# K and V caches in one array read in tiles across borders, and layer 1's output projection in other tile sizes with unread products between

## The chip, the cores and the metric

The kernel runs on one core of one Trainium2 chip. The metric is the device time of one execution in microseconds (us), the median of several runs. Before the change it is 847.03 us, the median of 3 runs that lie between 846.56 and 848.1.

## The reference, cut to what matters

Two decoder layers with the same weights, one new token for each of 8 batches. A layer is attention over a cache of 4096 positions (32 query heads, 4 K/V heads of 128), then an MLP with a GELU.

```
x = x + A(layernorm(x))      # B=8, Sq=1, D=1024
x = x + M(layernorm(x))
x = x + A(layernorm(x))      # the same K, V and weights a second time
x = x + M(layernorm(x))

A(x): q = (x @ wq) as [8, 32, 1, 128];  k, v = caches [8, 4, 4096, 128], each K/V head for 8 query heads
      softmax(q k^T * 128**-0.5) v, heads side by side, @ wo        # wo [4096, 1024]
M(x): gelu(x @ w1 + b1) @ w2 + b2                                   # w1 [1024, 3584], w2 [3584, 1024]
```

All of it is float32. The two caches are 67 MB each and are read once in each layer.

## The kernel before

**The arena.** One buffer in on-chip memory, `arena`, holds everything that comes from memory. It is cut into 52 places of `SCW` = 1024 columns (128 x 1024 float32, 512 KB). Place 51 belongs to the softmax rows; in layer 0 places 0 to 27 hold `wq`, which the end of layer 0 uses again for layer 1's queries.

**The stream.** `stream` is a list, written out by hand, of every transfer of the program: how many places, from where in memory, and at which place of the arena it goes. `pump` walks it in order and issues each entry on SP's queue as soon as its places have been given back; SP is the only engine that issues these transfers, so an entry that has no place holds back all behind it. `release` gives a tile's places back after the last product that reads them. The transfers themselves run one behind the other.

**Attention.** `plan` goes through the batches; for each batch 8 pieces of K (`scores`, 2 places each), then the softmax (`probs`), then 8 pieces of V (`values`, 2 places each). `ap_of` finds the piece in the tile that holds it. In layer 0 the batches go 0 to 7, in layer 1 they go 7 to 0, so that the V of batch 7 (`shared`) stays on the chip between the layers. K and V are two arrays; a tile is 8 or 4 places (4 or 2 pieces) of one batch's K or V and starts and ends at a border of K or V. In layer 0 the tiles move through places 28 to 47, in layer 1 mostly as tiles of 8 through places 18 to 41.

**Output projection.** `project` multiplies the heads' outputs with `wo`. One place of `wo` is one head: four products of 256 columns into the four strips of the sum `y`, which the trace shows as 8 rows, since a product in float32 is two rows there. In layer 0 `wo` comes in tiles of 3 places and after each tile `idle` puts products on TensorE whose result nobody reads. In layer 1 it comes in tiles of 8, 8, 8, 4, 2 and 2 places, and nothing is put between.

**Unread products.** `idle` and `unread` do the same: `unread(n)` issues n products of 512 columns into one strip of 32 partitions of a PSUM tile that is called `none`. Before the change it is called only at the start of layer 1's attention (two after each of four K pieces, four in `probs`).

**MLP of layer 1.** After `project` and `layernorm` the program calls `expand("i1", ...)`: `w1` comes in tiles of 4 places; 4 places are one group u of 512 hidden columns (the products of line 317, from u = 5 on line 320). The variance (the products of line 211) is computed half way through group 0; the result of a group is scaled on ScalarE (line 335), transposed on TensorE (line 413), added up on VectorE, put through GELU, and multiplied one group later with `w2` (line 497, `down_row`), all of which is on the chip but for three last pieces (`LATE`). The sum is added to the residual on VectorE (line 872) and written out.

Of the kernel before, what the change touches and what calls it, by code (L numbers as in the profile page):

```python
# [8 lines left out]
F32 = mybir.dt.float32  # L9
# [5 lines left out]
P = 128  # L15
# [10 lines left out]
NG = W // CH  # L26
T = CH // P
NR = NH * HKV
EPS = 1e-5
PAD = 24  # L30
SCALE = DH ** -0.5
# [21 lines left out]
LATE_AT = 20  # L53
LATE_C = 2
LATE = ((0, 2), (2, 1), (3, 1))
NGR = F // CH
# [56 lines left out]


@with_exitstack
def decode_layers(ctx: ExitStack, tc: tile.TileContext, x, kc, vc, wq, wo, w1, w2, out):


    nc = tc.nc
# [75 lines left out]
            nc.tensor.matmul(ps[0:32, 0:w], ident[:, 0:32], ap[:, 0:w], start=True, stop=True)  # L195

    def unread(n):
        idle(*[CH] * n, ps=ps_o.tile([P, CH], F32, tag="o", name="none"), ap=arena.ap)

    turns = {}  # L200

# [231 lines left out]
    def project(name, lhs, resid, rsum, hooks={}):  # L433
        y = ps_o.tile([P, CH], F32, tag="o", name="y")
        n = 0
        for slot in tiles((name,)):
            for c in range(0, slot.cols, D):
                for j in range(4):
                    nc.tensor.matmul(y[32 * j:32 * j + 32, 0:Q4], lhs[:, n * B:n * B + 32],  # L439
                                     slot.ap[:, c + j * Q4:c + (j + 1) * Q4],  # L440
                                     start=(n == 0), stop=(n == HQ - 1))
# [12 lines left out]

# [219 lines left out]

    def ap_of(key):

        parts = pieces[st["layer"], key] if (st["layer"], key) in pieces else pieces[0, key]
        chunks = [held[name].ap[:, c:c + CH] for name, c0, n in parts for c in range(c0, c0 + n, CH)]
        return chunks, [name for name, c0, n in parts if c0 + n == held[name].cols]

    def plan(order):

# [61 lines left out]
            stream.append(((name, i0 + i), k, dram[:, at:at + n], starts(k, i), keys))  # L744
            at += n

    def lane(layer, b, a, r, m):
        where = k_at if a == "k" else v_at
        keys = [(a, *where(b, e)) for e in range(r, r + m)]
        for e, key in enumerate(keys):  # L750
            pieces[layer, key] = [((layer, keys[0]), e * W, W)]
        return (layer, keys[0]), (kc if a == "k" else vc)[b][:, r * W:(r + m) * W]

    def cache(layer, b, a, at):
        r = 0
        while r < NR:
            n, starts = at(2 * (NR - r))
            name, src = lane(layer, b, a, r, n // 2)
            yield (name, n, src, starts, ())
            r += n // 2  # L760

    rsum = row_sums()
    nc.vector.tensor_reduce(rsum, x_row, AX.X, ALU.add)

    last_b = B - 1
    shared = (("v7", 1, 44), ("v7b", 7, 28), ("v7c", 4, 35), ("v7d", 4, 39))
    orders = [list(range(B)), list(range(B))[::-1]]

    def fixed(*at):
        return lambda k, i: (at[i],)  # L770
# [8 lines left out]
    def listed(*spots):  # L779
        spots = iter(spots)  # L780
        return lambda left: next(spots)

    def batch(layer, b, k_spots, v_spots):
        for a, spots in [(a, spots) for a, spots in (("k", k_spots), ("v", v_spots)) if spots]:
            stream.extend(cache(layer, b, a, listed(*((n, (at,)) for n, at in spots))))
# [3 lines left out]
    batch(0, 0, ((8, 40), (4, 32), (4, 36)), ((4, 28), (8, 40), (4, 32)))  # L789
    batch(0, 1, ((4, 36), (4, 28), (8, 40)), ((8, 32), (8, 40)))  # L790
    cycle = [(((8, 36), (4, 44), (4, 28)), ((8, 32), (8, 40))), (((8, 28), (4, 36), (4, 40)), ((4, 44), (8, 28), (4, 36))),
             (((8, 40), (8, 28)), ((4, 36), (8, 40), (4, 28))), (((8, 32), (8, 40)), ((8, 28), (4, 36), (4, 40))),
             (((4, 44), (8, 28), (4, 36)), ((8, 40), (8, 28)))]
    for b in orders[0][2:last_b]:
        batch(0, b, *cycle[(b - 1) % 5])
    batch(0, last_b, cycle[(last_b - 1) % 5][0], ())
    at = 0
    for name, k, to in shared:
        keys = [(1, name, e) for e in range(k)] if at else ()
        stream.append(((0, name), k, vc[last_b][:, at:at + k * SCW], (to,), keys))  # L800
        for e in range(k):
            key = ("v", *v_at(last_b, (at + e * SCW) // W))
            pieces.setdefault((0, key), []).append(((0, name), e * SCW, SCW))
            pieces.setdefault((1, key), []).append(((1, name, e), 0, SCW) if keys else ((1, name), 0, SCW))
        at += k * SCW
# [4 lines left out]
    stream.append(((1, "v7"), 1, vc[last_b][:, 0:SCW], (17,), ()))  # L810
    batch(1, last_b, ((2, 20), (2, 22), (4, 24), (2, 18), (2, 20), (2, 22), (2, 24)), ())
    batch(1, last_b - 1, ((2, 26), (2, 18), (4, 20), (2, 24), (2, 28), (4, 30)), ((8, 34), (8, 18)))
# [12 lines left out]
    for layer in range(2):  # L825
        st["layer"] = layer
        b2_row = spare[:, SCW:SCW + Q4]
        hooks = {("probs", last_b): opened} if layer == 0 else {
            ("v", *v_at(last_b - 2, 0)): lambda: bias_row(b2_row, spare[:, SCW + Q4:SCW + Q4 + CH]),
            ("v", *v_at(last_b - 1, 1)): rebuild,  # L830
            ("v", *v_at(last_b - 3, 0)): bias_diag,
            **{("k", *k_at(last_b, r)): lambda: unread(2) for r in range(NR - 4, NR)}}
        last = attention(orders[layer], hooks)
        rsum = row_sums()
        project(f"o{layer}", oT, x_row, rsum, {4: last})
        rs = layernorm(x_row, rsum)
        if layer == 0:
            idle(CH)
            expand("i0", rs)
            idle(CH, Q4)  # L840
            swap()
        else:
            nc.vector.tensor_tensor(x_row, x_row, b2_row, ALU.add)
            y = []
# [27 lines left out]
            nc.vector.tensor_tensor(x_row, x_row, y[0], ALU.add)  # L872
# [14 lines left out]
    return w.reshape(1, -1, P, D).transpose(0, 2, 1, 3).reshape(1, P, -1)  # L887


def _tiles(n):  # L890
    return [t for j in range(4) for t in range(j, n, 4)]

# [20 lines left out]
def _start(x, b1, b2):  # L913
# [3 lines left out]

_LAYOUT = {
    'x': (('A_x', 'B_b1', 'B_b2'), _start),
    'k': (('A_k_cache',), lambda a: a.reshape(B, HKV, 4, 32, NH, W // DH, DH).transpose(0, 6, 4, 1, 2, 5, 3).reshape(B, P, -1)),  # L920
    'v': (('A_v_cache',), lambda a: a.reshape(B, HKV, P, -1).transpose(0, 2, 1, 3).reshape(B, P, -1)),
    'wq': (('A_wq',), _queries),
    'wo': (('A_wo',), _down),
    'w1': (('B_w1',), _across),
# [24 lines left out]
```

## Time and profile before

| | |
|---|---|
| median of 3 runs | 847.03 us (846.56 to 848.1) |
| profiled execution | 849.2 us, its span from first to last instruction 847.3 us |
| mean granted TensorE clock | 0.827 of full speed |
| busy: TensorE, its weight loads, VectorE, ScalarE | 66%, 22%, 23%, 7% of the span |
| bytes read | 356.21 MB, 421 GB/s over the span |

A row of a timeline gives the start and the length in us, the engine (PE is TensorE, PEld its weight loads, DVE VectorE, ACT ScalarE, SP SyncE), the line of the kernel, the operation, the tile written and those read, the shape, the number of instructions, and in brackets the idle time before it with what ended it. A row of windows gives a stretch, its length, for each engine the busy time and the number of instructions, then the granted clock of TensorE (1.00 is full speed), the mean busy share of the 16 DMA engines, and GB/s. A row of the chain gives start, length, and what the end of the program was waiting for in that time.

### The profile page before, as it was taken

What the parts mean: (1) busy time and instruction counts of PE and PEld (TensorE: products, weight loads), DVE (VectorE), ACT (ScalarE), POOL (GpSimd) and SP (SyncE); (2) the same over time, 40 slices, a digit from 0 to 9 for tenths busy, and PEclk for the clock granted to TensorE, in tenths of its full rate; (3) what the DMA queues carried; (4) which work ended last, traced back from release to release, by engine and by line L of the source; (5) the groups of instructions that cost most, each with busy time, mean ns of one, the idle gap of its engine ahead of it and who ended that gap; (6) DMA issues with size and microseconds to landing.
All of it is one profiled execution on the core that took longest, in us unless ns stands there. A gap on an engine that the chain in (4) does not pass through costs nothing.

```text
span 847.3 us, 9962 instructions
## 1 busy us (share of the span) xinstructions
PE 557.7 (66%) x4350; PEld 188.9 (22%) x4350; DVE 193.4 (23%) x642; ACT 55.9 (7%) x118; POOL 2.4 (0%) x14
## 2 busy tenths in 40 slices
PE   0756475566656647688988796576765566665778
PEld 0211121111111112133244322121211111112335
DVE  0013131313223231300010343231314132222011
ACT  0110000000000000000210200000000000000021
POOL 0000000000000000000000000000000000000000
PEclk9977778867787877799999998867688877878679
DMA  9999999999999999999999999999999999999997
GB/s 402 420 424 429 433 422 425 438 425 434 422 430 438 422 439 420 418 414 416 411 407 411 411 409 432 435 429 431 429 433 428 435 431 428 435 425 431 424 425 283
DMA packets 21066, 356.97 MB, mean 421 GB/s; under 512 B 2336, under 2 KB 2720, under 8 KB 4256
## 3 DMA queue, kind: packets, MB, share of 16 engines
q1 hardware_dynamic: 20880, 356.20, 99.0%
q8 instruction: 34, 0.56, 0.3%
q10 hardware_dynamic: 144, 0.15, 0.1%
q14 instruction: 8, 0.07, 0.0%
HBM read 356.21 MB, written 0.13 MB: 421 GB/s over the span
## 4 chain that ended last, share of the span: by engine, by line
DMA 68%; PE 28%; DVE 1%; issue 1%; another core or an unknown queue 1%; ACT 0%; SPq 0%; ACTq 0%; DVEq 0%
DMA arena<-in_k_dram 27%; DMA arena<-in_v_dram 24%; PE sps L612 8%; PE o_ps L657 8%; DMA arena<-in_w_dram 6%; DMA arena<-in_wo_dram 6%; DMA arena<-in_wq_dram 5%; PE acc L376 2%; PE acc L317 2%; PE sps L497 1%; PE y L439 1%; PE sps L484 1%; PE none L195 1%; PE sps L669 1%; PE acc L320 1%
## 5 line engine op out<-in xcount | busy, mean ns | idle before, releaser
L612 PE MATMUL sps<-arena,qz 128*32 128x512 f32 x1024 | 168.7, 801 | 120.2 <-DMA arena<-in_k_dram 119.1
L657 PE MATMUL o_ps<-arena 128*32 128x512 f32 x512 | 88.6, 811 | 44.3 <-DMA arena<-in_v_dram 32.8
L657 PE MATMUL o_ps<-arena,spare 128*32 128x512 f32 x512 | 81.4, 746 | 37.4 <-DMA arena<-in_v_dram 35.1
L612 PEld LDWEIGHTS sps<-arena,qz 128*32 128x32 f32 x1024 | 38.7, 136 | 211.0 <-issue 176.4
L662 DVE SCALAR_TENSOR_TENSOR scr<-o_ps,bits,scr 128x128 f32<-128x128 f32 x192 | 67.4, 351 | 6.8
L660 DVE TENSOR_SCALAR scr<-o_ps,bits 128x128 f32<-128x128 f32 x64 | 22.5, 351 | 135.9 <-PE o_ps L657 135.9
L439 PE MATMUL y<-arena,oxT 128*32 128x256 f32 x512 | 38.4, 444 | 18.1 <-DMA arena<-in_wo_dram 18.1
L669 PEld LDWEIGHTS sps<-bits,scr 128*128 128x128 f32 x128 | 22.0, 216 | 70.1 <-issue 49.1
L376 PE MATMUL acc<-arena,oxT 128*32 128x512 f32 x248 | 33.2, 664 | 6.5 <-DMA arena<-in_wq_dram 4.2
L657 PEld LDWEIGHTS o_ps<-arena 128*32 128x32 f32 x512 | 17.2, 134 | 79.3 <-issue 49.3
L195 PE MATMUL sps<-spare,ident 128*32 128x512 f32 (+2 forms) x82 | 33.9, 533 | 1.1 <-DVE scr L231 0.6
L670 DVE TENSOR_TENSOR oxT<-sps,scr 128x8 f32<-128x8 f32 x64 | 10.6, 165 | 101.1 <-PE sps L669 101.1
L617 DVE TENSOR_SCALAR_CACHE_REDUCE arena<-sps 128x512 f32<-128x512 f32 x16 | 11.1, 692 | 90.8 <-PE sps L612 90.8
L657 PEld LDWEIGHTS o_ps<-arena,spare 128*32 128x32 f32 x512 | 17.2, 125 | 65.4 <-issue 45.4
L638 ACT ACTIVATE sps<-arena,bits 128x512 f32<-128x512 f32 x16 | 10.9, 681 | 283.5 <-DVE scr L632 283.5
L617 DVE TENSOR_SCALAR_CACHE_REDUCE spare<-sps 128x512 f32<-128x512 f32 x16 | 11.1, 692 | 79.8 <-PE sps L612 79.8
L317 PE MATMUL acc<-arena,oxT 128*32 128x512 f32 x160 | 26.7, 675 | 3.8 <-DMA arena<-in_w_dram 3.8
L638 ACT ACTIVATE sps<-spare,bits 128x512 f32<-128x512 f32 x16 | 10.9, 681 | 266.1 <-DVE scr L632 266.1
L669 PE MATMUL sps<-bits,scr 128*128 128x8 f32 x128 | 27.9, 290 | 0.0
L439 PEld LDWEIGHTS y<-arena,oxT 128*32 128x32 f32 x512 | 17.2, 126 | 40.6 <-DMA arena<-in_wo_dram 24.0
L626 PE MATMUL sps<-scr,bits 128*128 128x128 f32 x32 | 7.4, 312 | 21.4 <-DVE scr L622 21.4
L220 PE MATMUL sps<-ident,xb 128*128 128x128 f32 x6 | 1.5, 344 | 24.2 <-DMA xb<-in_x_dram 23.2
(138 smaller groups left out, 285.3 us busy)
## 6 DMA issues: line engine op xcount, KB each, us to landing
arena<-in_v_dram SPq DMA_DIRECT2D x24, 4096.0 KB, 21.9
arena<-in_k_dram SPq DMA_DIRECT2D x22, 4096.0 KB, 21.3
arena<-in_k_dram SPq DMA_DIRECT2D x15, 2048.0 KB, 18.2
arena<-in_v_dram SPq DMA_DIRECT2D x10, 2048.0 KB, 18.6
arena<-in_wo_dram SPq DMA_DIRECT2D x10, 1536.0 KB, 9.8
arena<-in_w_dram SPq DMA_DIRECT2D x10, 1536.0 KB, 8.5
arena<-in_w_dram SPq DMA_DIRECT2D x12, 1024.0 KB, 9.8
arena<-in_w_dram SPq DMA_DIRECT2D x6, 2048.0 KB, 21.9
```

What stands on the lines that cost most here:

```text
L195: nc.tensor.matmul(ps[0:32, 0:w], ident[:, 0:32], ap[:, 0:w], start=True, stop=True)
L317: nc.tensor.matmul(acc[32 * j:32 * j + 32, :], lhs, slot.ap[:, c:c + CH], start=(kt < 4), stop=(kt >= NT - 4))
L376: nc.tensor.matmul(acc[u][32 * j:32 * j + 32, d0 - j * CH:d1 - j * CH], xnT[:, kt * XS:kt * XS + 32], ap[:, d0 - c0:d1 - c0], start=(kt == ...
L439: nc.tensor.matmul(y[32 * j:32 * j + 32, 0:Q4], lhs[:, n * B:n * B + 32], slot.ap[:, c + j * Q4:c + (j + 1) * Q4], start=(n == 0), stop=(n ...
L612: nc.tensor.matmul(ps[32 * g:32 * g + 32, :], qz[:, c:c + 32], kt[g], start=(j == 0), stop=(j == HKV - 1))
L617: nc.vector.tensor_scalar(st["row", b].ap[:, half * CH:(half + 1) * CH], ps, SCALE, None, op0=ALU.mult, op1=ALU.max, accum_out=st["mx", b] ...
L638: nc.scalar.activation(pp, row[:, h * CH:(h + 1) * CH], AF.Exp, bias=bias, scale=1.0, accum_out=ls[:, h:h + 1])
L657: nc.tensor.matmul(o[32 * g:32 * g + 32, :], s[:, g], v[g], start=(half == 0), stop=(half == NH - 1))
L660: nc.vector.tensor_scalar(r, o[:, 0:P], sel_t[:, 0:1], None, op0=ALU.mult)
L662: nc.vector.scalar_tensor_tensor(r, o[:, t * P:(t + 1) * P], sel_t[:, t:t + 1], r, op0=ALU.mult, op1=ALU.add)
L669: nc.tensor.matmul(po[:, 0:REP], r_s[j % 2], sel_h, start=True, stop=True)
L670: nc.vector.tensor_tensor(oT_v[:, j * REP:(j + 1) * REP, b], po[:, 0:REP], rl_s[b % 2][:, j * REP:(j + 1) * REP], ALU.mult)
```

## The change

K and V are one array `kv`: row p holds batch after batch that partition's K and then its V, 256 places in all, and behind them one place of zeros that no transfer reads. `cache` cuts this row into tiles without regard to the borders of pieces, of K and V, or of batches; `pieces` notes for each piece which places of which tiles hold it, and a tile is given back after the last piece that it has a part of.

- Layer 0: tiles of 8, 7 and 8 places in turn at places 36, 44 and 28 (23 places against 20), then 2, 1, 7, 4 and 4.
- Layer 1: the batches go 7, 0, 1, ..., 6, so that the array is read upwards. After the same first tiles as before come tiles of 9, 9 and 8 places in turn at 34, 17 and 26 (26 places against 24).
- Layer 1's `wo`: tiles of 8, 8, 8, 6 and 2 at 34, 17, 26, 34 and 40. After the third tile (24 heads) stand ten unread products, after the fourth (30 heads) two, and behind the layernorm four.
- `w1` in layer 1 has its old sizes at other places, `LATE` lies at place 22 instead of 20.

```
+            elif n < HQ:
+                unread({3 * HQ // 4: 10, HQ - 2: 2}.get(n, 0))
...
-    orders = [list(range(B)), list(range(B))[::-1]]
+    orders = [list(range(B)), [last_b, *range(last_b)]]
...
+    low, mid, high = (8, 28), (8, 36), (7, 44)
+    g = cache(0, 0, [mid, high, low] * 10 + [mid, (2, 46)])
+    g = cache(0, g, ((1, 44),))
+    cache(0, g, ((7, 28), (4, 35), (4, 39)), part=True)
...
-    at = [26, 34, 18] * (4 * B)
-    for b in orders[1][2:]:
-        batch(1, b, *([(8, at.pop(0)), (8, at.pop(0))] for _ in "kv"))
-    weights(("o1",), wo[0], [8, 8, 8, 4, 2, 2], fixed(26, 34, 18, 26, 30, 32))
-    weights(("i1",), w1[0], [4] * 5 + [2] * 3 + [1, 0.5, 0.5], fixed(34, 38, 18, 22, 26, 30, 32, 34, 36, 37, 38))
+    low, mid, high = (9, 17), (8, 26), (9, 34)
+    cache(1, 0, [(2, 26), (2, 18), (4, 20), (2, 24), (2, 28), (4, 30), high, low] + [mid, high, low] * 7 + [mid])
+    weights(("o1",), wo[0], [8, 8, 8, 6, 2], fixed(34, 17, 26, 34, 40))
+    weights(("i1",), w1[0], [4] * 5 + [2] * 3 + [1, 0.5, 0.5], fixed(17, 21, 26, 30, 34, 38, 40, 17, 19, 20, 21))
...
         else:
+            unread(4)
             nc.vector.tensor_tensor(x_row, x_row, b2_row, ALU.add)
...
+def _cache(k, v):
...
+    rows = _np.concatenate([k, v], 2).transpose(1, 0, 2).reshape(P, -1)
+    return _np.concatenate([rows, _np.zeros((P, SCW), _np.float32)], 1)
```

How the instructions stand shows it at three places (columns of a transfer: 1024 are one place; in brackets the semaphores that the instruction waits for, DMAHW are those of earlier transfers). First SP's queue at the start of layer 0's caches, before:

```order
L282 DMA arena<-in_k_dram 128x8192
L282 DMA arena<-in_k_dram 128x4096 x2
L282 DMA arena<-in_v_dram 128x4096 [waits DMAHW0_49,DVE_49,DMAHW4_49,PE_49,Activation_49]
L282 DMA arena<-in_v_dram 128x8192 [waits DMAHW5_49,DMAHW1_49,PE_49]
L282 DMA arena<-in_v_dram 128x4096 [waits DMAHW6_49,DMAHW2_49,PE_49]
L282 DMA arena<-in_k_dram 128x4096 [waits DMAHW7_49,DMAHW3_49,PE_49]
L282 DMA arena<-in_k_dram 128x4096 [waits DMAHW0_49,PE_49]
L282 DMA arena<-in_k_dram 128x8192 [waits DMAHW1_49,PE_49]
```

The same place after the change:

```order
L284 DMA arena<-in_kv_dram 128x8192
L284 DMA arena<-in_kv_dram 128x7168
L284 DMA arena<-in_kv_dram 128x8192 [waits DVE_49,DMAHW4_49,PE_49,Activation_49]
L284 DMA arena<-in_kv_dram 128x8192 [waits DMAHW5_49,DMAHW0_49,PE_49]
L284 DMA arena<-in_kv_dram 128x7168 [waits DMAHW6_49,DMAHW1_49,PE_49]
L284 DMA arena<-in_kv_dram 128x8192 [waits DMAHW7_49,DMAHW2_49,PE_49]
```

Every tile is now 7 or 8 places; over layer 0 SP issues 36 transfers for the caches where it issued 44, and over layer 1 it issues 38 where it issued 40.

Second SP's queue at layer 1's `wo`, before:

```order
L282 DMA arena<-in_wo_dram 128x8192 [waits DMAHW2_49,PE_49]
L282 DMA arena<-in_wo_dram 128x8192 [waits DMAHW3_49,PE_49]
L282 DMA arena<-in_wo_dram 128x8192 [waits DMAHW4_49,PE_49]
L282 DMA arena<-in_wo_dram 128x4096 [waits DMAHW5_49,PE_49]
L282 DMA arena<-in_wo_dram 128x2048 [waits PE_49] x2
```

and after:

```order
L284 DMA arena<-in_wo_dram 128x8192 [waits DMAHW0_49,PE_49]
L284 DMA arena<-in_wo_dram 128x8192 [waits DMAHW1_49,PE_49]
L284 DMA arena<-in_wo_dram 128x8192 [waits DMAHW2_49,PE_49]
L284 DMA arena<-in_wo_dram 128x6144 [waits DMAHW3_49,PE_49]
L284 DMA arena<-in_wo_dram 128x2048 [waits PE_49]
```

The tiles of 4 and 2 places have become one of 6.

Third TensorE's order from the end of the third `wo` tile to the start of `w1`'s group 0 (line 439 and 441 are `project`, 211 and 213 the mean and the variance, 317 and 319 `expand`; here a product is one row), before:

```order
L439 MATMUL y<-arena,oxT 32x256 x11
L439 MATMUL y<-arena,oxT 32x256 [waits DMAHW0_49]
L439 MATMUL y<-arena,oxT 32x256 x15
L439 MATMUL y<-arena,oxT 32x256 [waits DMAHW1_49]
L439 MATMUL y<-arena,oxT 32x256 x7
L439 MATMUL y<-arena,oxT 32x256 [waits DMAHW2_49]
L439 MATMUL y<-arena,oxT 32x256 x7
L220 MATMUL sps<-ident,xb 128x128 [waits DVE_49]
...
L211 MATMUL sps<-bits 32x1 x3
L317 MATMUL acc<-arena,oxT 32x512 [waits DMAHW3_49,DVE_49,PE_49]
```

and after:

```order
L441 MATMUL y<-arena,oxT 32x256 x11
L196 MATMUL none<-arena,ident 32x512 [waits PE_49]
L196 MATMUL none<-arena,ident 32x512 x9
L441 MATMUL y<-arena,oxT 32x256 [waits DMAHW6_49]
L441 MATMUL y<-arena,oxT 32x256 x23
L196 MATMUL none<-arena,ident 32x512 [waits PE_49]
L196 MATMUL none<-arena,ident 32x512
L441 MATMUL y<-arena,oxT 32x256 [waits DMAHW7_49]
L441 MATMUL y<-arena,oxT 32x256 x7
...
L213 MATMUL sps<-bits 32x1 x3
L196 MATMUL none<-arena,ident 32x512 [waits PE_49]
L196 MATMUL none<-arena,ident 32x512 x3
L319 MATMUL acc<-arena,oxT 32x512 [waits DMAHW0_49,DVE_49,PE_49]
```

Ten, two and four products stand ahead of work that was next in line before; they wait for nothing but TensorE.

More of the change, by code (lines that the diff above doesn't have):

```diff
@@ L28 @@
 NR = NH * HKV
+RU = 2 * NR
 EPS = 1e-5
@@ L52 @@
         ("w2", 11, 6, 0, 4), ("w2", 12, 6, 4, 16), ("q", 6, 1), ("w2", 13, 6, 20, 8), ("x", 6))
-LATE_AT = 20
+LATE_AT = 22
 LATE_C = 2
@@ L115, in decode_layers @@
 @with_exitstack
-def decode_layers(ctx: ExitStack, tc: tile.TileContext, x, kc, vc, wq, wo, w1, w2, out):
+def decode_layers(ctx: ExitStack, tc: tile.TileContext, x, kv, wq, wo, w1, w2, out):
     nc = tc.nc
@@ L197, in unread @@
     def unread(n):
-        idle(*[CH] * n, ps=ps_o.tile([P, CH], F32, tag="o", name="none"), ap=arena.ap)
+        if n:
+            idle(*[CH] * n, ps=ps_o.tile([P, CH], F32, tag="o", name="none"), ap=arena.ap)
     turns = {}
@@ L675, in ap_of @@
     def ap_of(key):
-        parts = pieces[st["layer"], key] if (st["layer"], key) in pieces else pieces[0, key]
-        chunks = [held[name].ap[:, c:c + CH] for name, c0, n in parts for c in range(c0, c0 + n, CH)]
-        return chunks, [name for name, c0, n in parts if c0 + n == held[name].cols]
+        parts = [part for _, part in sorted(pieces[st["layer"], key].items())]
+        chunks = [held[name].ap[:, c + e:c + e + CH] for name, c in parts for e in range(0, SCW, CH)]
+        return chunks, [name for name, c in parts if c + SCW == held[name].cols]
     def plan(order):
@@ L745, in weights, with cache @@
             at += n
[L747 to L760, printed above, removed]
+    def cache(layer, g, spots, part=None):
+        for k, at in spots:
+            name = (layer, "kv", g)
+            keys = [(1, "kv", g + e) for e in range(k)] if part else ()
+            stream.append((name, k, kv[:, g * SCW:(g + k) * SCW], (at,), keys))
+            for e in range(k):
+                b, r = divmod(g + e, 2 * RU)
+                a, r = "kv"[r // RU], r % RU // 2
+                key = (a, *(k_at if a == "k" else v_at)(b, r))
+                pieces.setdefault((layer, key), {})[g + e] = name, e * SCW
+                if part:
+                    pieces.setdefault((1, key), {})[g + e] = keys[e], 0
+            g += k
+        return g
     rsum = row_sums()
@@ L777, in down_weights @@
             c0 += cols
[L779 to L785, printed above, removed]
     halves = lambda i: [[("q", kt, u) for kt in kts for u in range(2)] for kts in ((0, 1, 2, 3), (4, 5), (6,), ())][i]
     weights(("q0",), wq[0], [16, 8, 4, 4], fixed(0, 16, 24, 28), kept=halves)
[L789 to L805, printed above, removed]
+    low, mid, high = (8, 28), (8, 36), (7, 44)
+    g = cache(0, 0, [mid, high, low] * 10 + [mid, (2, 46)])
+    g = cache(0, g, ((1, 44),))
+    cache(0, g, ((7, 28), (4, 35), (4, 39)), part=True)
     weights(("o0",), wo[0], [3, 2] + [3] * 9, fixed(*[46, 49, 43] * 4))
@@ L809, in decode_layers @@
     stream.append((("qe", 0), 0, wq[0][:, -W:-KEEP], x_row[:, 0:W - KEEP], ()))
-    stream.append(((1, "v7"), 1, vc[last_b][:, 0:SCW], (17,), ()))
-    batch(1, last_b, ((2, 20), (2, 22), (4, 24), (2, 18), (2, 20), (2, 22), (2, 24)), ())
-    batch(1, last_b - 1, ((2, 26), (2, 18), (4, 20), (2, 24), (2, 28), (4, 30)), ((8, 34), (8, 18)))
-    at = [26, 34, 18] * (4 * B)
-    for b in orders[1][2:]:
-        batch(1, b, *([(8, at.pop(0)), (8, at.pop(0))] for _ in "kv"))
-    weights(("o1",), wo[0], [8, 8, 8, 4, 2, 2], fixed(26, 34, 18, 26, 30, 32))
-    weights(("i1",), w1[0], [4] * 5 + [2] * 3 + [1, 0.5, 0.5], fixed(34, 38, 18, 22, 26, 30, 32, 34, 36, 37, 38))
+    first = last_b * 2 * RU
+    cache(1, first + RU, ((1, 17),))
+    cache(1, first, ((2, 20), (2, 22), (4, 24), (2, 18), (2, 20), (2, 22), (2, 24)))
+    low, mid, high = (9, 17), (8, 26), (9, 34)
+    cache(1, 0, [(2, 26), (2, 18), (4, 20), (2, 24), (2, 28), (4, 30), high, low] + [mid, high, low] * 7 + [mid])
+    weights(("o1",), wo[0], [8, 8, 8, 6, 2], fixed(34, 17, 26, 34, 40))
+    weights(("i1",), w1[0], [4] * 5 + [2] * 3 + [1, 0.5, 0.5], fixed(17, 21, 26, 30, 34, 38, 40, 17, 19, 20, 21))
     for e, n in LATE:
@@ L828, in decode_layers @@
         hooks = {("probs", last_b): opened} if layer == 0 else {
-            ("v", *v_at(last_b - 2, 0)): lambda: bias_row(b2_row, spare[:, SCW + Q4:SCW + Q4 + CH]),
-            ("v", *v_at(last_b - 1, 1)): rebuild,
-            ("v", *v_at(last_b - 3, 0)): bias_diag,
+            ("v", *v_at(orders[1][2], 0)): lambda: bias_row(b2_row, spare[:, SCW + Q4:SCW + Q4 + CH]),
+            ("v", *v_at(orders[1][1], 1)): rebuild,
+            ("v", *v_at(orders[1][3], 0)): bias_diag,
             **{("k", *k_at(last_b, r)): lambda: unread(2) for r in range(NR - 4, NR)}}
@@ L887, in _down @@
     return w.reshape(1, -1, P, D).transpose(0, 2, 1, 3).reshape(1, P, -1)
+def _cache(k, v):
+    import numpy as _np
+    k = k.reshape(B, HKV, 4, 32, NH, W // DH, DH).transpose(0, 6, 4, 1, 2, 5, 3).reshape(B, P, -1)
+    v = v.reshape(B, HKV, P, -1).transpose(0, 2, 1, 3).reshape(B, P, -1)
+    rows = _np.concatenate([k, v], 2).transpose(1, 0, 2).reshape(P, -1)
+    return _np.concatenate([rows, _np.zeros((P, SCW), _np.float32)], 1)
 def _tiles(n):
@@ L919 @@
     'x': (('A_x', 'B_b1', 'B_b2'), _start),
-    'k': (('A_k_cache',), lambda a: a.reshape(B, HKV, 4, 32, NH, W // DH, DH).transpose(0, 6, 4, 1, 2, 5, 3).reshape(B, P, -1)),
-    'v': (('A_v_cache',), lambda a: a.reshape(B, HKV, P, -1).transpose(0, 2, 1, 3).reshape(B, P, -1)),
+    'kv': (('A_k_cache', 'A_v_cache'), _cache),
     'wq': (('A_wq',), _queries),
```

1 line of the change is left out of this document (removed).

## The prediction

> **What bounds the kernel now.** I read the page first, then windows, then TensorE's timeline and the chain for the last 60 us. The page's rows on the queues say what sets the pace (packets, MB, share of the span that 16 DMA engines were busy with them):
>
> ```profile
> span 847.3 us, 9962 instructions
> ...
> q1 hardware_dynamic: 20880, 356.20, 99.0%
> q8 instruction: 34, 0.56, 0.3%
> ```
>
> SP's queue keeps the DMA engines busy for 99.0% of 847.3 us, 838.8 us; 8.5 us are left for the start, the end and every gap in 847 us together. So more buffer can win a few us at the most. What is left to win in the transfers is their rate. The windows show it for layer 0's caches, for tiles of 2 places, and for layer 1's tiles of 8; behind them stand stretches of the end (the last two columns are the DMA share and GB/s, the one before is TensorE's granted clock):
>
> ```profile
> 100.00:340.00 240.00, 148.68 (x872) 41.60 (x872) 62.73 (x205) 9.11 (x24) 0.00 (x0) 0.76 1.00 429
> 476.00:500.00 24.00, 20.43 (x114) 6.03 (x113) 7.42 (x27) 3.45 (x8) 0.00 (x0) 1.00 1.00 418
> 580.00:740.00 160.00, 98.25 (x576) 28.45 (x576) 42.27 (x137) 6.07 (x16) 0.00 (x0) 0.78 1.00 431
> ...
> 794.40:801.20 6.80, 5.63 (x56) 2.64 (x60) 0.00 (x0) 0.00 (x0) 0.00 (x0) 0.50 0.99 412
> 801.20:808.00 6.80, 5.20 (x92) 2.72 (x84) 0.73 (x4) 0.00 (x0) 0.00 (x0) 1.00 1.04 441
> 808.00:818.30 10.30, 7.03 (x40) 2.11 (x44) 1.66 (x7) 4.45 (x8) 0.00 (x0) 0.50 1.00 422
> 818.30:844.00 25.70, 25.25 (x450) 15.54 (x442) 2.99 (x12) 4.13 (x10) 0.00 (x0) 1.00 0.87 358
> ```
>
> Up to about 800 us TensorE is busy for 0.6 of the time and the DMA share is 1.00: there the transfers are the bound and TensorE has room. From 818.3 on it is the other way: TensorE is busy for 25.25 of 25.70 us at full clock. Its timeline there:
>
> ```profile
> 785.84 6.18 PE L439 MATMUL y<-arena,oxT 128*32 128x256 f32 x64 [4.03 <-DMA arena<-in_wo_dram]
> 795.57 9.02 PE L439 MATMUL y<-arena,oxT 128*32 128x256 f32 x112 [3.55 <-DMA arena<-in_wo_dram]
> 805.44 1.07 PE L439 MATMUL y<-arena,oxT 128*32 128x256 f32 x16 [0.84 <-DMA arena<-in_wo_dram]
> ...
> 807.56 0.24 PE L211 MATMUL sps<-bits 128*32 128x1 f32 x8
> 810.42 1.94 PE L317 MATMUL acc<-arena,oxT 128*32 128x512 f32 x8 [2.62 <-DMA arena<-in_w_dram]
> 812.10 0.32 PE L211 MATMUL sps<-bits 128*32 128x1 f32 x8
> ...
> 815.02 1.12 PE L413 MATMUL sps<-ident,scr 128*128 128x128 f32 x4 [0.85 <-ACT scr L335]
> 816.07 3.01 PE L317 MATMUL acc<-arena,oxT 128*32 128x512 f32 x16
> ...
> 820.74 0.66 PE L413 MATMUL sps<-ident,scr 128*128 128x128 f32 x4
> ...
> 822.16 1.92 PE L317 MATMUL acc<-arena,oxT 128*32 128x512 f32 x16
> ```
>
> TensorE last waits for a transfer at 810.42 (`w1`'s group 0). From group 1 at 816.07 no row names a transfer any more; the chain goes along TensorE to the end:
>
> ```profile
> 841.39 2.76 PE sps L497 x46
> 844.15 0.02 issue
> 844.17 0.42 DVE xb L872
> ```
>
> So from 816.07 to 844.15, 28.08 us, whatever delays TensorE delays the end by as much. Two bounds follow one another: transfers, then TensorE; the change touches both.
>
> **The change part by part.** The sum is made against the profiled execution (849.2 us, span 847.3); the median of the runs is 2.17 us lower, and I carry the difference over to it.
>
> *Fewer transfers.* The bytes are the same, the place of zeros is not read. A place is 0.524 MB. A tile of 2 takes 1.049 MB / 418 GB/s = 2.51 us, so four take 10.03; one of 8 takes 4.194 / 431 = 9.73. Three issues saved are worth 0.30 us, 0.10 each. Layer 0 has 44 - 36 = 8 fewer, layer 1's caches 2, `wo` 1; the first ten lie ahead of `wo`'s third tile: **-1.0 us**. Bounds: 0, if the 418 comes from something else in that stretch; 1.9, if the windows' 429 of layer 0's 313 us became 431 (1.5) and the rest comes on top.
>
> *Tiles across borders and more places.* A tile that ends inside a piece is given back only when its successor has landed and the piece has been multiplied. The rows on how early a tile must be issued (issue to landing, from the chain):
>
> ```profile
> 116.95 14.67 DMA arena<-in_k_dram
> ...
> 556.65 24.06 DMA arena<-in_k_dram
> ...
> 610.00 3.60 PE o_ps L657 x16
> ```
>
> The tile of 116.95 takes 9.73 by itself and was issued 4.9 us before its turn, with the DMA share at 1.00 all through that window; in layer 1 it is usually 14. After the change a tile is issued, at the worst, one piece (8 rows of V, half of 3.60, 1.8 us) after the landing of the next one, with one more of 7 to 9 places (8.5 to 10.9 us) still in flight: 6.7 to 9 us ahead. That is above 4.9: **0 us**, hidden behind the tile in flight. Without this cover every border would cost its shortfall (a rival below). The upward order of batches moves no transfer's size and no bound: 0.
>
> *The unread products.* Their price stands in the chain at layer 1's start, where the clock is full and each `unread(2)` is 4 rows:
>
> ```profile
> 485.64 1.67 PE none L195 x4
> 487.31 0.86 PE sps L612 x8
> 488.16 1.72 PE none L195 x4
> ```
>
> 1.69 us for two, 0.85 each; all go into one strip, one behind the other. Ten are 8.5 us, two 1.7, four 3.4. The tenths: the third `wo` tile is followed by a tile of 6 places, 3.146 MB / 431 = 7.3 us later, and one of 2, 2.5 us after that. TensorE needs 6.18 us for 8 heads (row of 785.84), so a gap of about 1.1 us opens before the fourth tile, and ten products of 8.5 are put into it.
>
> The end, step by step in the time of the profile: third tile starts 795.57 - 1.0 = 794.6; eight heads 6.2 to 800.8; ten products 8.5 to 809.3; by then both last tiles have landed (801.9 and 804.4), so no wait is left to hide anything. Six heads at full clock, (9.02 - 6.18)/6 = 0.47 each, 2.8 to 812.1; two products 1.7 to 813.8; two heads 1.1 to 814.9. Before, this point was 806.51 (805.44 + 1.07): **+8.4 us**. To the end of the mean (807.56 + 0.24) 807.80 - 806.51 = 1.3: 816.2. Four products 3.4: 819.6, where group 0 starts (before 810.42; its tile has long landed, so the 2.62 us that TensorE idled before it are used up). Half of group 0 at full clock is half of 1.92, 1.0: 820.6 for the variance. From the variance to the transposes it takes 815.02 - 812.10 = 2.9 us through ScalarE: 823.5, and 0.6 for them: group 1 at 824.1 instead of 816.07. From there 28.08 us, less 3.01 - 1.92 = 1.1, since the products keep TensorE busy and I take the full clock that the row of 801.20 got after one busy stretch: 27.0, end at 851.1 instead of 844.15. **+6.9 us**, the 1.0 of the transfers already in it.
>
> Bounds of this term: if the third tile is consumed at full clock, 8 x 0.47 = 3.8 instead of 6.2, -2.4; if two of the ten products still run at half the clock, +1.7; the transfers' 0 to -1.9 add +1.0 or -0.9. So +3.6 to +9.6. I take the middle sum because 6.18 is the row of the tile just ahead, in the same place of the program.
>
> *The rest.* `w1`'s tiles at other places wait for heads that are consumed later. The last to be issued needs group 1, 824.1 and a little, and the transfers of `w1` are still running then (28 places, 34 us from 804): hidden. The late tiles at place 22 need the same group: 0.
>
> Sum: 849.2 + 6.9 = 856.1 for the profiled execution, **853.9 us** for the median.
>
> A rule of the Trainium skill speaks for the change here. TensorE: Matmul & The Clock Gate, section on the back-to-back issue gap, gives N / 2.4 + 2.5 ns for a warm product of N columns, 216 ns for 512; ten would be 2.2 us and would end at 803.0, before the fifth tile lands, and the sum would be the first rival's below. The trace does not agree, 850 ns for this product in float32, and the measurement decides.
>
> **The rivals.**
>
> *The products fit into the waits, and the warm clock pays.* The end is not later if group 1 starts by 844.15 - 27.0 = 817.2, that is `y` by 817.2 - 9.2 = 808.0. From 800.8 with 2.8 + 1.1 for the heads, 3.3 us are left for twelve products, 0.28 each. Against it stands 0.85 in three rows; for it only that those rows come from another stage. The end would then hang on the last transfers: -1.1 for fewer issues and up to 1 of the queue that TensorE works off now, 845.5 us, no change or just faster.
>
> *The new rows cost DMA rate.* A partition's row is now 257 x 4 KB, against 64 KB within one batch. The caches are (256 + 225) x 0.524 = 252 MB, 585 us; each percent of rate costs 5.9 us, and 5% would give 883. Against it: rows of 128 KB (`wo`) run no slower than those of 64 KB, the window at 794.40 to 808.00 has 412 and 441.
> [...]
>
> *Borders starve the queue.* If a tile has to be issued 9 us ahead and not 4.9, up to 2 us are lost at most of 36 borders in layer 0, some 40 us, 894 us. Against it the share of 1.00 around 116.95.
>
> **How the numbers follow.** My forecast 0.83, own range 850 to 857; products that fit 0.10; row pitch 0.04; starved queue 0.03. To hold 8 in 10 the range must hold nearly all of the forecast, and it takes in cases where the products are half hidden: 849.0 to 857.5. A measurement of this kernel can tell about 0.2%, 1.7 us. Slower by more: the forecast, the pitch, the starved queue, less the few cases where the forecast's sum is far too large: 0.87. Within: most of the second case, 0.09. Faster by more: what is left of it, 0.04.
>
> **What the profile after would show.** The span about 854; the same 356.2 MB on queue 1 with 11 fewer issues; 431 GB/s in both layers' caches with a share of 1.00. In TensorE's timeline 20 rows of `none` in about 8.5 us after the third `wo` tile, and the rows of `y` behind them waiting for no transfer; `y` done 7 to 9 us later, group 1 at about 824, the clock at 1.00 from 801 to the end, the last transfer landed some 8 us before the last product. Wrong it is if `none` takes under 0.4 us each, if a row of `y` behind it still waits for `wo`, if group 1 starts before 818, or if the DMA share in the caches falls below 0.99.

## The result, and the profile after

The changed kernel takes 852.36 us (median of 6 runs, 851.54 to 853.61), the kernel before 847.13 us beside it (6 runs, 845.9 to 848.1): ratio 1.0063, 95% interval 1.0050 to 1.0076. It is slower by 5.2 us. The kernel before was run again beside each experiment; its medians there lie between 846.99 and 847.96 us, so it is the ratio to it that is compared. The profiled execution of after took 851.54 us, 0.8 below its median.

The page's rows on span and queues come first (packets, MB, share of the span):

```profile
span 849.8 us, 9971 instructions
...
q1 hardware_dynamic: 19296, 356.20, 98.4%
```

The bytes are the same in fewer packets. 98.4% of 849.8 us are 836.2 us of transfers, 13.6 us are left for gaps, 5.1 more than before. The windows of the same stretches show where (the last three columns are granted clock, DMA share and GB/s):

```profile
100.00:340.00 240.00, 155.12 (x880) 40.42 (x877) 63.20 (x206) 9.11 (x24) 0.00 (x0) 0.77 1.00 431
580.00:740.00 160.00, 96.22 (x568) 25.12 (x568) 42.28 (x137) 6.07 (x16) 0.00 (x0) 0.81 1.00 430
794.40:801.20 6.80, 6.80 (x50) 2.60 (x43) 0.00 (x0) 0.00 (x0) 0.00 (x0) 0.88 0.98 412
801.20:808.00 6.80, 6.80 (x59) 2.51 (x57) 0.00 (x0) 0.00 (x0) 0.00 (x0) 1.00 1.00 426
808.00:818.30 10.30, 9.09 (x70) 2.96 (x65) 1.91 (x8) 3.16 (x5) 0.00 (x0) 1.00 1.01 428
818.30:844.00 25.70, 24.22 (x418) 15.10 (x422) 3.15 (x13) 5.09 (x13) 0.00 (x0) 1.00 0.74 301
840.00:850.00 10.00, 6.64 (x160) 4.38 (x152) 0.87 (x3) 0.46 (x2) 0.00 (x0) 1.00 0.04 15
```

The caches run at 431 and 430 GB/s with a share of 1.00, as before. From 794.4 to 808 TensorE is now busy without a break where it was for 5.63 and 5.20 of 6.80 us. Behind 840 the DMA engines have nothing left (0.04), while TensorE works on: the gaps stand at the end of the program. TensorE's timeline there:

```profile
792.05 5.35 PE L441 MATMUL y<-arena,oxT 128*32 128x256 f32 x64 [4.38 <-DMA arena<-in_wo_dram]
797.21 8.32 PE L196 MATMUL none<-arena,ident 128*32 128x512 f32 x19
804.95 0.63 PE L441 MATMUL y<-arena,oxT 128*32 128x256 f32 x6
805.37 0.59 PE L196 MATMUL none<-arena,ident 128*32 128x512 f32 x1
805.80 2.75 PE L441 MATMUL y<-arena,oxT 128*32 128x256 f32 x42
808.39 1.45 PE L196 MATMUL none<-arena,ident 128*32 128x512 f32 x3
...
810.10 1.03 PE L441 MATMUL y<-arena,oxT 128*32 128x256 f32 x10
...
812.28 3.17 PE L196 MATMUL none<-arena,ident 128*32 128x512 f32 x7
814.87 0.63 PE L319 MATMUL acc<-arena,oxT 128*32 128x512 f32 x3
...
819.33 0.66 PE L415 MATMUL sps<-ident,scr 128*128 128x128 f32 x4 [1.66 <-ACT scr L337]
819.91 1.92 PE L319 MATMUL acc<-arena,oxT 128*32 128x512 f32 x16
```

A product is two rows here: 19 and 1 are the ten (six rows of `y` are recorded ahead of their last row), 3 and 1 the two, 7 and 1 the four. The last row that waits for a transfer is that of 792.05; no `y` and no `acc` behind the products waits for one. The chain goes through them from there to the end:

```profile
797.40 7.95 PE none L196 x19
...
812.44 3.01 PE none L196 x7
...
844.01 2.68 PE sps L501 x48
846.68 0.02 issue
846.71 0.42 DVE xb L855
```

### The profile page after: what moved, and what is told of

Same layout as the page of the kernel before. It is cut to its first block, busy times and chain, and to the rows that moved or that the text cites. A ratio compares the mean times of both kernels' runs of the same rounds, so it can differ in the third digit from the quotient of the medians.

```text
span 849.8 us, 9971 instructions
## 1 busy us (share of the span) xinstructions
PE 569.7 (67%) x4382; PEld 186.2 (22%) x4382; DVE 193.4 (23%) x642; ACT 55.6 (7%) x118; POOL 2.4 (0%) x14
## 3 DMA queue, kind: packets, MB, share of 16 engines
q1 hardware_dynamic: 19296, 356.20, 98.4%
## 4 chain that ended last, share of the span: by engine, by line
DMA 58%; PE 34%; DVE 4%; ACT 2%; issue 1%; SPq 0%; ACTq 0%; DVEq 0%
DMA arena<-in_kv_dram 41%; PE o_ps L661 12%; DMA arena<-in_wo_dram 8%; PE sps L616 7%; DMA arena<-in_wq_dram 5%; DMA arena<-in_w_dram 4%; PE none L196 3%; PE y L441 2%; PE acc L378 1%; PE sps L501 1%; PE acc L319 1%; PE sps L488 1%; ACT sps L642 1%; PE sps L630 1%; PE sps L673 1%
## 5 line engine op out<-in xcount | busy, mean ns | idle before, releaser
L616 PE MATMUL sps<-arena,qz 128*32 128x512 f32 x1024 | 173.7, 768 | 115.4 <-DMA arena<-in_kv_dram 114.4
L661 PE MATMUL o_ps<-arena,spare 128*32 128x512 f32 x512 | 84.6, 750 | 39.4 <-DMA arena<-in_kv_dram 25.6
L616 PEld LDWEIGHTS sps<-arena,qz 128*32 128x32 f32 x1024 | 35.9, 131 | 215.0 <-DMA arena<-in_kv_dram 126.7
L441 PE MATMUL y<-arena,oxT 128*32 128x256 f32 x512 | 36.5, 414 | 17.7 <-DMA arena<-in_wo_dram 17.7
L378 PE MATMUL acc<-arena,oxT 128*32 128x512 f32 x248 | 30.8, 623 | 7.1 <-DMA arena<-in_wq_dram 4.7
L196 PE MATMUL none<-arena,ident 128*32 128x512 f32 x56 | 25.4, 592 | 0.0
L319 PE MATMUL acc<-arena,oxT 128*32 128x512 f32 x160 | 24.7, 600 | 1.0 <-DMA arena<-in_w_dram 1.0
```

What stands on the lines that cost most here:

```text
L319: nc.tensor.matmul(acc[32 * j:32 * j + 32, :], lhs, slot.ap[:, c:c + CH], start=(kt < 4), stop=(kt >= NT - 4))
L378: nc.tensor.matmul(acc[u][32 * j:32 * j + 32, d0 - j * CH:d1 - j * CH], xnT[:, kt * XS:kt * XS + 32], ap[:, d0 - c0:d1 - c0], start=(kt == ...
L616: nc.tensor.matmul(ps[32 * g:32 * g + 32, :], qz[:, c:c + 32], kt[g], start=(j == 0), stop=(j == HKV - 1))
L661: nc.tensor.matmul(o[32 * g:32 * g + 32, :], s[:, g], v[g], start=(half == 0), stop=(half == NH - 1))
```

## The experiments

The theory is that the products alone make the loss, because sixteen of 0.85 us (13.6 us) stand in one strip on the path and only a part of it finds a wait to fill. Rivals are the rows of `kv` (pitch), the cut of the caches, and the tiles of `wo`. All kernels compute the whole output; what differs is the unread work, tiles or places.

**The products taken out of the changed kernel.**

```diff
-                unread({3 * HQ // 4: 10, HQ - 2: 2}.get(n, 0))
+                unread(0)
...
-            unread(4)
+            unread(0)
```

> The changed kernel without its sixteen unread products in layer 1 (ten, two and four); array, tiles and order of batches as changed. Theory (the products stand on the path that sets the end, 0.85 us each): the loss goes and the transfers' gain of 1 to 3 us stays, 844 to 846.5 us; in the trace the sum of the output projection waits for its last tile again and group 0 of w1 for its transfer. Rival (the tiles across borders or the longer rows cost the time, the products are hidden): it stays at 851 to 853 us.

846.80 us (10 runs, 845.03 to 848.56), ratio to before 0.9980, interval 0.9966 to 0.9993. The loss is gone; the time is 0.3 us above the range that I expected, so less came of the transfers than I thought. TensorE's timeline of this kernel at the end:

```profile
800.27 5.35 PE L441 MATMUL y<-arena,oxT 128*32 128x256 f32 x64 [2.13 <-DMA arena<-in_wo_dram]
...
807.74 1.07 PE L319 MATMUL acc<-arena,oxT 128*32 128x512 f32 x8 [0.83 <-DMA arena<-in_w_dram]
...
811.73 0.65 PE L415 MATMUL sps<-ident,scr 128*128 128x128 f32 x4 [2.00 <-ACT scr L337]
812.55 1.93 PE L319 MATMUL acc<-arena,oxT 128*32 128x512 f32 x16 [0.16 <-DMA arena<-in_w_dram]
...
822.34 1.92 PE L319 MATMUL acc<-arena,oxT 128*32 128x512 f32 x16 [0.55 <-DMA arena<-in_w_dram]
...
827.25 1.92 PE L319 MATMUL acc<-arena,oxT 128*32 128x512 f32 x16 [0.63 <-DMA arena<-in_w_dram]
...
838.41 2.81 PE L501 MATMUL sps<-arena,oxT 128*32 128x256 f32 x45
```

The waits for `w1` are back (0.83, 0.16, 0.55, 0.63): TensorE follows the transfers again. That is the sign of which bound holds: with products no row behind 792 waits for a DMA, without them five do.

The two profiles also tell where the products' time goes. In the chain of the changed kernel they hold TensorE for 13.2 us. Against that, the five waits for transfers (2.13, 0.83, 0.16, 0.55 and 0.63 us) are gone, and the last eight heads take 4.0 us there, at full clock, instead of 5.35. That leaves 7.5 us; counted from the start of the third tile, the last product ends 6.2 us later (54.6 against 48.4). The remaining 1.3 us I did not trace.

**The end alone, on the kernel before** (its arrays, tiles and order of batches kept; `wo` in 8, 8, 8, 6, 2 and the products added).

```diff
+            elif n in (3 * HQ // 4, HQ - 2):
+                unread({3 * HQ // 4: 10, HQ - 2: 2}[n])
...
-    weights(("o1",), wo[0], [8, 8, 8, 4, 2, 2], fixed(26, 34, 18, 26, 30, 32))
+    weights(("o1",), wo[0], [8, 8, 8, 6, 2], fixed(26, 34, 18, 26, 32))
...
+            unread(4)
```

> The kernel before with only the end of the change: layer 1's output projection in tiles of 8, 8, 8, 6 and 2 and the unread products (ten, two, four). Theory: the loss without the transfers' gain, 6 to 8 us over before, 853 to 855.5 us. Rival (the loss comes from the caches' tiles): 846.5 to 848 us.

853.96 us (6 runs, 853.33 to 857.34), ratio 1.0076, interval 1.0058 to 1.0094. The end alone makes the whole loss; the interval overlaps that of the changed kernel. Its timeline, third `wo` tile, ten products and group 1:

```profile
792.99 6.23 PE L439 MATMUL y<-arena,oxT 128*32 128x256 f32 x64 [3.74 <-DMA arena<-in_wo_dram]
799.04 8.32 PE L195 MATMUL none<-arena,ident 128*32 128x512 f32 x19
...
821.74 1.92 PE L317 MATMUL acc<-arena,oxT 128*32 128x512 f32 x16
```

19 rows take 8.32 us here too. The third tile starts at 792.99, 2.6 us earlier than in the profile of before, though nothing ahead of it is changed: so much does one execution differ from another at this place.

**Five products instead of ten.**

```diff
-                unread({3 * HQ // 4: 10, HQ - 2: 2}.get(n, 0))
+                unread({3 * HQ // 4: 5, HQ - 2: 2}.get(n, 0))
```

> The changed kernel with five unread products after the third tile of the output projection instead of ten; two and four as changed. Theory (each product that is not in a wait delays the end by 0.86 us): five times 0.86 = 4.3 us less than the changed kernel, 848.1 us (847.3 to 849). Rival (what costs is that the products are there at all, by the order of the work or by the clock, and not their number): within 1 us of the changed kernel, over 851 us.

849.09 us (8 runs, 847.85 to 850.48), ratio 1.0026, interval 1.0016 to 1.0036. Timeline:

```profile
793.26 5.30 PE L441 MATMUL y<-arena,oxT 128*32 128x256 f32 x64 [4.68 <-DMA arena<-in_wo_dram]
798.39 4.03 PE L196 MATMUL none<-arena,ident 128*32 128x512 f32 x9
...
816.80 1.93 PE L319 MATMUL acc<-arena,oxT 128*32 128x512 f32 x16
```

Group 1 starts 23.5 us behind the third tile's start, with ten products 27.9 (819.91 - 792.05): 4.3 us for five, 0.86 each. The time is just above the 847.3 to 849 us that I expected. By the ratios five products less are worth 3.1 us, and at the ends of the two intervals 1.2 or 5.1, so 4.3 is not excluded. In the two profiled executions the spans differ by 2.9 us (849.8 and 846.9), since this one's third tile starts 1.2 us later.

**The same sixteen products, spread over four strips.** Operands and PSUM tile are the same; only the output strip of each goes round 0, 32, 64, 96.

```diff
+    def spread(n):
+        ps = ps_o.tile([P, CH], F32, tag="o", name="none")
+        for i in range(n):
+            at = 32 * (i % 4)
+            nc.tensor.matmul(ps[at:at + 32, 0:CH], ident[:, 0:32], arena.ap[:, 0:CH], start=True, stop=True)
...
-                unread({3 * HQ // 4: 10, HQ - 2: 2}.get(n, 0))
+                if n in (3 * HQ // 4, HQ - 2):
+                    spread({3 * HQ // 4: 10, HQ - 2: 2}[n])
...
-            unread(4)
+            spread(4)
```

> The changed kernel with its sixteen unread products spread over the four strips of 32 partitions of their PSUM tile instead of all in the first. Theory (products into one strip stand one behind the other, those into four strips run beside each other): ten take some 2.6 us instead of 8.5, two and four 0.9 each, so nearly all of them fit into the waits: 846 to 848 us. Rival (a product takes its 0.85 us of TensorE wherever it goes): 851.5 to 853.5 us.

846.38 us (12 runs, 844.97 to 851.10), ratio 0.9998, interval 0.9983 to 1.0013: no loss with as many products. Timeline, the ten, the four and group 3:

```profile
799.39 2.31 PE L202 MATMUL none<-arena,ident 128*32 128x512 f32 x18
...
807.59 1.05 PE L202 MATMUL none<-arena,ident 128*32 128x512 f32 x8
...
822.98 1.93 PE L325 MATMUL acc<-arena,oxT 128*32 128x512 f32 x16 [0.47 <-DMA arena<-in_w_dram]
```

18 rows take 2.31 us instead of 8.32 for 19, and the wait for `w1` is there again. So it is neither the number of products nor their semaphores, but the time that they hold one strip. The Trainium skill, TensorEngine Tiling (Array Packing), section Key Properties, says that tiles of the array run independently and in parallel; with about a quarter of the time these rows agree.

**Three products, none, three**: enough to fill the waits and no more.

```diff
-                unread({3 * HQ // 4: 10, HQ - 2: 2}.get(n, 0))
+                unread({3 * HQ // 4: 3}.get(n, 0))
...
-            unread(4)
+            unread(3)
```

> The changed kernel with three unread products after the third tile of the output projection instead of ten, none after the fourth and three behind the layernorm instead of four: as many as fit into the waits that the traces show there (2.5 us before the fourth tile, 2.6 us before group 0). Theory: nothing is delayed, TensorE enters group 0 at full clock and follows the transfers, so the end hangs on the last transfer: 844 to 846 us, 0.3 to 1.5 us under the kernel without products. Rival (the warm clock is worth nothing, since TensorE catches up anyway): within 0.3 us of the kernel without products.

847.23 us (11 runs, 845.89 to 852.42), ratio 0.9999, interval 0.9983 to 1.0014. The products cost nothing, and the gain that I expected of a warm clock did not come. Its timeline, and a window of the stretch behind:

```profile
811.66 0.66 PE L415 MATMUL sps<-ident,scr 128*128 128x128 f32 x4 [1.64 <-ACT scr L337]
812.93 3.58 PE L319 MATMUL acc<-arena,oxT 128*32 128x512 f32 x16 [0.61 <-DMA arena<-in_w_dram]
```

```profile
813.00:816.50 3.50, 3.50 (x20) 1.18 (x24) 0.00 (x0) 0.19 (x1) 0.00 (x0) 0.51 0.99 421
```

Between the products and group 1 stand the waits for ScalarE (1.64) and for the next tile (0.61), and group 1 runs at a granted clock of 0.51, 3.58 us instead of 1.92. In this execution the products ahead of the waits did not keep the clock behind them. It is not a matter of their length alone: the kernel without products had waits of 2.00 and 0.16 us at the same place, and its group 1 ran at full clock, 1.93 us. What decides between the two is not shown.

**The caches' part alone**: the changed kernel without products and with `wo` cut as before.

```diff
-                unread({3 * HQ // 4: 10, HQ - 2: 2}.get(n, 0))
+                unread(0)
...
-    weights(("o1",), wo[0], [8, 8, 8, 6, 2], fixed(34, 17, 26, 34, 40))
+    weights(("o1",), wo[0], [8, 8, 8, 4, 2, 2], fixed(34, 17, 26, 34, 38, 40))
...
-            unread(4)
+            unread(0)
```

> The changed kernel without the unread products in layer 1 and with the output projection in the tiles of before (8, 8, 8, 4, 2, 2): only the one array, its tiles and the order of batches are left of the change. Theory (fewer transfers, the tiles of wo matter little): 846 to 847.5 us, within 0.5 us of the kernel with 8, 8, 8, 6, 2 and no products. Rival (it is the tile of 6 that keeps TensorE's clock up and gave the gain): 1 us or more above that one, 847.5 to 848.5 us.

848.03 us (12 runs, 846.05 to 851.22), ratio 1.0006, interval 0.9993 to 1.0019. That lies in the rival's range, but the ratio is that of no change: ten issues fewer are not to be seen in the time. Timeline, the last wait for `wo` and group 0:

```profile
804.12 1.07 PE L441 MATMUL y<-arena,oxT 128*32 128x256 f32 x16 [1.41 <-DMA arena<-in_wo_dram]
...
809.12 1.93 PE L319 MATMUL acc<-arena,oxT 128*32 128x512 f32 x8 [2.63 <-DMA arena<-in_w_dram]
```

TensorE waits at the same two places as in the kernel before (0.84 and 2.62 us there). The two runs so far left open whether the tile of 6 was worth something, 0.9980 with it against 1.0006; two more kernels ask that.

**The `wo` tiles alone, and once more the changed kernel without products.** The first is the kernel before with this line, the second is unchanged from above.

```diff
-    weights(("o1",), wo[0], [8, 8, 8, 4, 2, 2], fixed(26, 34, 18, 26, 30, 32))
+    weights(("o1",), wo[0], [8, 8, 8, 6, 2], fixed(26, 34, 18, 26, 32))
```

> The kernel before with one line changed: layer 1's wo in tiles of 8, 8, 8, 6, 2 at places 26, 34, 18, 26, 32, no products, caches as before. Theory: the tile of 6 lets eight heads run through at full clock and group 0 follow warm, which was worth 1 to 2 us in the run without products; then 845 to 846.5 us, ratio 0.997 to 0.999. Rival: the gain there was chance in the phase of the clock or came only with the new caches; then 847 to 848 us, no difference from before.

> The changed kernel without the unread products once more, beside the wo tiles alone. If its gain over the kernel before is real, 845 to 847 us, ratio 0.997 to 0.999 again; if it was chance, 847 to 848 us.

The `wo` tiles alone take 847.14 us (12 runs, 845.80 to 848.07), ratio 0.9995, interval 0.9981 to 1.0008; the changed kernel without products 846.98 us (12 runs, 845.37 to 852.36), ratio 0.9997, interval 0.9981 to 1.0012. The first lies in its rival's range; the second stands on the border of the two times that I named, and its ratio is that of chance. The gain of 0.9980 was not seen again: that kernel's medians are 846.80 and 846.98, the difference lay in the kernel before, 847.96 beside the first and 846.99 beside the second. Timelines, the `wo` tiles alone first:

```profile
800.41 3.66 PE L439 MATMUL y<-arena,oxT 128*32 128x256 f32 x64 [2.22 <-DMA arena<-in_wo_dram]
...
807.89 1.94 PE L317 MATMUL acc<-arena,oxT 128*32 128x512 f32 x8 [2.53 <-DMA arena<-in_w_dram]
```

and the changed kernel without products, second time:

```profile
791.80 6.17 PE L441 MATMUL y<-arena,oxT 128*32 128x256 f32 x64 [3.81 <-DMA arena<-in_wo_dram]
799.52 3.66 PE L441 MATMUL y<-arena,oxT 128*32 128x256 f32 x64 [1.55 <-DMA arena<-in_wo_dram]
...
806.84 1.67 PE L319 MATMUL acc<-arena,oxT 128*32 128x512 f32 x8 [2.38 <-DMA arena<-in_w_dram]
```

The last eight heads do run through in one, and `y` is done at 804.1 and 803.2; but group 0 then waits 2.53 and 2.38 us for `w1`, so nothing is gained: the transfers set this end. Apart from that one comparison, no version that was tried is measurably faster than the kernel before.

**The place of zeros taken away**, rows exactly 1 MiB apart. If the distance of the rows cost rate, the windows of the caches would show it.

```diff
-    return _np.concatenate([rows, _np.zeros((P, SCW), _np.float32)], 1)
+    return rows
```

> The changed kernel without the place of zeros behind each partition's row of the one array, so that the rows lie exactly 1 MiB apart. [...] Rival (the DMA engines' own pace is the bound at any pitch): 851 to 854 us, packets as long as in the changed kernel.

853.67 us (4 runs, 852.02 to 855.75), ratio to before 1.0065, interval 1.0046 to 1.0083: that of the changed kernel. The windows of both caches:

```profile
100.00:340.00 240.00, 150.62 (x876) 40.41 (x880) 63.18 (x206) 9.11 (x24) 0.00 (x0) 0.78 1.00 430
580.00:740.00 160.00, 98.31 (x568) 26.12 (x568) 42.27 (x137) 6.07 (x16) 0.00 (x0) 0.79 1.00 430
```

430 GB/s without the zeros, 431 and 430 with them: the pitch is out as a rival. The Trainium skill, DMA: Bandwidth & Descriptors, section Latency and other measured facts, reports for copies between HBM tensors 207 GB/s at a row pitch of 512 KiB, 164 at 2 MiB and 103 at 4 MiB, and 214 when the 4 MiB are padded by 4 KiB. These transfers are loads at 1 MiB, which it does not list, and the two rows above show no loss for them.

**Layer 0's caches in two places in turn instead of three**: the cover that I named for the borders is taken away.

```diff
-    g = cache(0, 0, [mid, high, low] * 10 + [mid, (2, 46)])
+    g = cache(0, 0, [(8, 36), (7, 28)] * 15 + [(8, 36), (7, 28)])
```

> The changed kernel with layer 0's caches in two tiles in turn (8 and 7 places) instead of three, so that a tile is issued only when the one after it has landed and been begun: the cover of the tile in flight is gone. Theory (a transfer must be issued some 4 us before its turn): each of some 31 tiles costs 1 to 2 us of piece and 3 us of start, 970 to 1010 us. Rival (an issue takes effect at once): 31 times 1.3 us over the changed kernel, about 892 us.

912.5 us, one run: 60 us over the changed kernel, between what both expected. The window of layer 0's caches, a short one inside it, and a piece of the chain (start, us, what):

```profile
100.00:340.00 240.00, 129.31 (x712) 33.61 (x704) 52.85 (x174) 7.59 (x20) 0.00 (x0) 0.71 0.86 356
```

```profile
125.00:131.00 6.00, 4.99 (x26) 1.38 (x30) 2.96 (x8) 0.92 (x4) 0.00 (x0) 0.57 0.00 0
```

```profile
130.22 1.01 PE o_ps L661 x6
131.25 12.36 DMA arena<-in_kv_dram
143.60 0.14 issue
143.74 3.62 PE o_ps L661 x16
```

The queue does starve: share 0.86 instead of 1.00, and from 125 to 131 us the DMA engines move nothing. A tile of 8 places that is issued only when its predecessor's last product is done (131.25) lands 12.36 us later, where 9.73 are its transfer (4.194 MB at 431 GB/s); the 4 us ahead that my expectation took for a need were too many, 2.6 fit this row. In the rest of the 60 us are the softmax's and the borders' waits, which I did not separate.

## Why the prediction was right, point by point

The sign, the place and the price were right; the time came out 1.5 us below the forecast (852.36 against 853.9) and inside the range, the loss 5.2 us where 6.9 were forecast. The profile was missed by more: its execution took 851.54 us where the sum gave 856.1, `y` was done 4.7 us later than before (811.2 against 806.51) and not 7 to 9, and group 1 started at 819.9 and not at 824.

- **The products, 0.85 us each, all on the path**: shown. 19 rows take 8.32 us in two kernels, five products less move group 1 by 4.3 us, and a quarter of the price removes the loss. In the chain the ten products, six heads, two products and two heads run from 797.40 to 811.20; that is 13.8 us, as 8.5 + 2.8 + 1.7 + 1.1 = 14.1 were to be.
- **No wait left to hide them**: shown. No row behind 792.05 waits for a transfer, with the products; without them the waits of `wo` and `w1` come back. A part of the products only replaces those waits: six in one strip cost nothing (0.9999), eleven cost 2.2 us by the ratio (1.0026), sixteen 5.3 (1.0063).
- **Eight heads 6.2**: too large in the profile of after, 5.35; in other runs the same row is 6.23 and 6.17, so the term is one of a single execution. One program gave both (the kernel without products, 5.35 and 6.17). The Trainium skill, TensorE: Matmul & The Clock Gate, Part 1, says that the number of slow products varies from run to run with the phase of a free-running window; these rows agree. The bound of -2.4 covered it.
- **Transfers -1.0**: mis-sized. By the caches' part alone it is nothing measurable, 1.0006 (0.9993 to 1.0019), so the bound of 0 was the better value: 0.10 us for each issue, taken from the 418 GB/s of one stretch, was not the price of an issue. The row of after starts the third tile at 792.05, 3.5 us earlier than before's, which looks like more than predicted; but the end alone and the `wo` tiles alone, with before's caches, have it at 792.99 and 792.85. One profile of each could not carry that difference.
- **Borders and more places 0**: the share of 1.00 in both windows agrees, and the starved run shows that the third tile in turn is the cover, as named. The cover was thinner than the 6.7 to 9 us that I worked out: the shortest time from issue to landing in layer 0 was 14.9 us (the tile issued at 196.63), 5.2 more than its 9.73. The 4.9 that I compared it with was not the least that is enough either: in the kernel before, the V tile issued at 109.13 landed after 12.8 us, so it was issued 3.1 ahead of its turn, in a stretch with a share of 1.00. The upward order showed no cost; it was not tried by itself.
- **The mean 1.3, four products 3.4, group 1 to the end 27.0**: 1.24 (811.20 to 812.44), 3.4 (3.01 + 0.39), and 26.7 (819.98 to 846.68) at clock 1.00. These terms held, and everything stands 3.7 to 4.4 us earlier, because the third tile and its heads did: 2.55 and 0.85.
- **From profile to median**: I carried over 2.17 us because before's profile lay that far above its median. After's lies 0.8 below. The offset is one of an execution, not of the kernel: before's profile caught a late third tile (795.57, against the 792.99 and 792.85 above), and taking 2.17 off the sum took most of that lateness off again without my knowing it. That the median came within 1.5 us, while the profile was missed by 4.6, is in this part luck.
- **The first rival**, products that fit into the waits, needed `y` by 808.0; it was done at 811.2. It became true where the price was a quarter: in four strips `y` was done at 806.4. **Row pitch and starved queue** did not act in this change: both caches' windows have a share of 1.00 and 431 and 430 GB/s (429 and 431 before), and the run without zeros has 430. The 252 MB in the first of them were a slip: the page's issue rows of the changed kernel add up to 497 places for the caches, 260.6 MB, 605 us at 431 GB/s; each percent would have cost 6.0 us and not 5.9.

## What to carry to other kernels

Before unread work is put ahead of work on the path, compare its length with the wait that it is to fill, and note which strip it holds: ten products of 0.85 us into one strip are 8.5 us, into four strips some 2.6. Where TensorE and the transfers set the end in turn, the timeline's brackets tell which one does: as long as a late group still waits for a DMA, TensorE has slack, and when the last such bracket goes, every further us on it is a us of the end. A gain of 0.2% in one comparison deserves a second one before it is explained.

## What the runs showed of the hardware

- Products of one shape into four strips ran side by side: 18 rows in 2.31 us against 19 in 8.32.
- A granted clock of 1.00 fell to 0.51 behind waits of 1.64 and 0.61 us with one short stretch of work between them (three products, none, three), while in the changed kernel a wait of 1.66 us, and in the kernel without products waits of 2.00 and 0.16 us, left group 1 at full clock (1.92 and 1.93 us).
- Rows 1 MiB apart were read at 430 GB/s, as with 4 KiB between them.
- A transfer of 4.2 MB that was issued when the DMA engines had run empty landed 12.36 us later, 2.6 more than the 9.73 us that it takes at the 431 GB/s of a full queue.
